# Chunk-selected attention and a top-1 mixture of experts: gate rows on four column tiles, rows beside scales, a one-operation freeze, a reordered prologue, and zero writes at other rounds

## The chip, the cores and the metric

The kernel runs on one core of a Trainium2 chip. Its engines are TensorE (PE, matrix products; PEld is its weight load), VectorE (DVE), ScalarE (ACT), GpSimd (POOL) and SyncE (SP, which here only issues transfers). They run side by side and wait for each other through semaphores. Products go to PSUM[...]; everything else that is computed on lies in SBUF. The metric is the device time of one execution in microseconds (us), lower being better.

## What is computed

The reference is attention over selected chunks, followed by a mixture of experts. Cut to what matters:

```python
# attention: q, k, v are (4, 8, 768, 64)
k_min, k_max = per chunk of 32 keys
ub = sum_d max(q * k_min, q * k_max)          # bound of each query on each chunk
ub = where(causal, ub, -1e9); top_chunks = best 6 of 24
attn = softmax(where(chunk selected and key <= query, q @ k.T / 8, -1e9))
x = (attn @ v) as 3072 tokens of 512
# experts: 8, capacity 80, w1 (512, 1024), w2 (1024, 512)
expert = argmax(x @ w_gate); gate = softmax(x @ w_gate)[expert]
per expert: keep the 80 tokens with the largest gate
out[kept] = gate * (relu(x[kept] @ w1[e]) @ w2[e]);  out[all others] = 0
```

So almost all rows of the output are zero and are written as such; at most 640 rows come from the experts.

## The kernel before, in words

**Tiling.** Four heads make a *quad*; there are 8 quads, two to a batch. The 768 queries of a quad are three tiles t of 256. A *round* is one tile against one pair of key blocks of 128, six rounds to a quad, 48 in all (`rd`, from 0). A tile's last round is an *end*; ends are at r = 0, 2 and 5 of a quad, and each starts a chain of follow-up work, described below.

**A round.** `score(rd)` puts products of rounded queries and keys (`QB`, `KB`) into four PSUM tiles (L459) and adds a large negative penalty to chunks that were not selected (L463, from `PENT` and the indicator `ind`). `exps(rd)` takes exponentials on ACT (L474) and cuts the causal triangle on POOL (L479); `sum_pairs` adds two blocks on POOL (L503) so that the denominators need half of the products. One round later, `value(rd - 1)` multiplies by v (L492, on four column tiles of the array, 32 columns each), `denom(rd - 1)` sums (L517), and at an end `evacuate` copies the numerators to SBUF (L523, `npt`).

**Follow-up of an end.** Two rounds after it `gate_rows` multiplies the numerators by the gate's weights into the PSUM tile that holds the denominators (L530: two products of 128x32 weights by 256 columns, on two column tiles), and ACT copies the result (L534, `DSB`). Three rounds after it `scales` transposes this (L542, `ps_dT`), and VectorE takes reciprocals and scaled gate logits; for the second quad of a batch `best` (L579 to 608) finds the maximum and a one-hot of the expert. Four rounds after it `rows` transposes the numerators (L564, `ps_xn`), scales them into `x_nat` on VectorE (L565) and stores them to `x_dram` through SP (L573). `gates` (L610) finishes the gate weight, and `merges` sort gates in lanes on VectorE (L661 to 722).

**Selection of chunks.** For each quad, `step` transposes k and q on VectorE (L262) and hands rounding and positive parts to POOL (L287) and ACT (L296, L301); `bound_all` and `rank_all` (L390 to 410) bound and rank all chunks, `unselect` (L417) makes the penalty. For quad 0 this is done in thirds in the prologue and in rounds 0 and 1: `keys_third`, `queries_third`, `bound`, `rank` (L355 to 377). The tiles `kT`, `qT`, `qp` have one buffer each, so a quad's first transpose waits until the quad before has been read.

**Freeze.** During rounds 44 to 47 a generator (L735 to 827) chooses the older tokens of batches 0 to 2: a threshold `tau`, prefix counts (`ps_cum`), a one-hot of the slot for each token (L775, 18 operations of 128x80), a product that gathers the kept ones (`ps_old`, L780), a transpose (`ps_gT`) and an exact ranking (`ps_all`). `turn_new` and the three `weigh` steps (L832 to 990) place batch 3's tokens; then the experts' rows are gathered (L1163), multiplied and scattered to `out` (L1205).

**Order and buffers.** The order on each engine is the order in which the program calls the functions, written out by hand (L1028 to 1160), since the planner is switched off there. Small products of all kinds take turns in two PSUM buffers of the pool `psM` (the function `misc`): a product waits until the one before last in that rotation has been read. `late` and `bulk` are lists of small operations that are put off until `flush`. `zero_fill` (L133) writes 512 KB of zeros to the output through SP, twelve times in even rounds 16 to 38. Weights for late experts are read by POOL's queue into tiles that have fallen free (`late_weights`, L999).

## Time and profile before

| | us |
|---|---|
| Median of three runs | 304.55 (301.02 to 305.59) |
| The profiled execution, whole | 302.78 |
| Its span, first to last instruction | 301.1 |
| TensorE busy, of the span | 264.2 (88%) |
| VectorE / ScalarE / GpSimd busy | 200.8 / 154.3 / 196.5 |
| Mean TensorE clock, of full | 0.964 |
| Gate-row products (L530, 96 records) | 15.9 |
| The 18 selection operations (L775) | 4.9 |
| Zero writes (12 of 512 KB), issue to landing | 7.8 each |

All of it but the first row is one execution under the profiler. A group's busy time sums durations that may overlap on TensorE, where tiles of the array run at once, so that records and not instructions are counted there. In the strips of the page a digit is the tenths of a slice of 7.5 us, and the clock strip shows the tenths of full clock that were granted. In a timeline a line has start, duration, engine, line, operation, operands, shapes and count, and in brackets how long the engine had waited and for what.

### The profile page before, as it was taken

Reading aid. Unit: us, or ns where it says so; the run is one execution under the profiler, and the core shown is the slowest. Engines: PE = TensorE matmul, PEld = TensorE weight load, DVE = VectorE, ACT = ScalarE, POOL = GpSimd, SP = SyncE. Lnnn points to the kernel's source line nnn. Section 1 sums busy time; section 2 is a strip of 40 time slices with the busy share of each in tenths; the row PEclk is TensorE's granted clock in tenths of the full one; section 3 lists DMA queues with packets and bytes.
Section 4 is the critical chain, followed back from the end, with each engine's and each line's share of the span. In section 5 each row is a group of like instructions: output and inputs, shape, how many; then the busy total and the mean of one; then the engine's idle time right before and its main releaser. Section 6 shows DMA issues by size and latency. Waiting matters only on the chain.

```text
span 301.1 us, 12164 instructions
## 1 busy us (share of the span) xinstructions
PE 264.2 (88%) x5026; PEld 157.1 (52%) x5026; DVE 200.8 (67%) x747; ACT 154.3 (51%) x352; POOL 196.5 (65%) x398
## 2 busy tenths in 40 slices
PE   8859799979998999799999989997994969789991
PEld 3426456646564666455565545564652544246760
DVE  3849458566746836699877989896989484632431
ACT  1553746934682685567468626856543244403220
POOL 8296695966995885699688739987794401155322
PEclk9999799999999999999999999999998699769999
DMA  7878903999899999999999999966999401112121
GB/s 168 157 191 132 198 6 84 208 166 146 184 204 274 177 217 263 259 190 243 228 272 189 244 257 206 231 102 119 187 214 205 95 3 35 35 44 69 47 65 35
DMA packets 59239, 47.79 MB, mean 159 GB/s; under 512 B 27846, under 2 KB 51526, under 8 KB 59184
## 3 DMA queue, kind: packets, MB, share of 16 engines
q1 hardware_dynamic: 45328, 28.09, 39.6%
q0 software_dynamic: 13536, 18.67, 36.2%
q8 instruction: 39, 0.64, 0.9%
q10 hardware_dynamic: 320, 0.26, 0.3%
q14 instruction: 16, 0.13, 0.1%
HBM read 53.10 MB, written 10.76 MB: 212 GB/s over the span
## 4 chain that ended last, share of the span: by engine, by line
PE 54%; DVE 17%; issue 11%; POOL 7%; ACT 5%; DMA 3%; SPq 2%; POOLq 1%; ACTq 0%; DVEq 0%
PE ps_num L492 20%; PE ps_den L517 8%; PE ps_S L459 6%; PE ps_u L390 6%; ACT E L474 4%; PE ps_den L530 4%; PE ps_xn L564 4%; DVE cand L666 3%; DVE cand L664 3%; PE ps_S L463 2%; POOL X L1163 2%; POOL out_dram L1205 2%; PE ps_dT L542 2%; DVE cand L775 2%; DMA qn<-in_q_dram 1%
## 5 line engine op out<-in xcount | busy, mean ns | idle before, releaser
L474 ACT ACTIVATE E<-ps_S 128x384 f32<-128x384 f32 (+1 forms) x192 | 88.7, 552 | 35.3 <-PE ps_S L463 35.3
L492 PE MATMUL ps_num<-E,vn 128*32 128x256 f32 (+1 forms) x1536 | 94.7, 361 | 3.8 <-issue 3.5
L503 POOL TENSOR_TENSOR both<-E 128x256 f32<-128x256 f32 x92 | 64.5, 731 | 15.6 <-ACT E L474 15.4
L492 PEld LDWEIGHTS ps_num<-E,vn 128*32 128x32 f32 x1536 | 50.4, 111 | 35.3 <-issue 9.7
L479 POOL TENSOR_SCALAR_AFFINE_SELECT E<-E 128x256 f32<-128x256 f32 x96 | 42.3, 468 | 34.0 <-ACT E L474 34.0
L459 PE MATMUL ps_S<-QB,KB 32*128 32x256 bf16 (+1 forms) x768 | 35.2, 261 | 3.0 <-ACT E L474 1.5
L534 ACT ACTIVATE DSB<-ps_den 128x256 f32<-128x256 f32 x24 | 9.2, 384 | 41.3 <-PE ps_den L530 37.8
L463 PE MATMUL ps_S<-PENT,ind 32*128 32x256 bf16 (+1 forms) x384 | 24.9, 255 | 2.5 <-DVE PENT L377 2.5
L459 PEld LDWEIGHTS <-KB 32*128 32x128 bf16 x768 | 17.2, 94 | 15.7 <-issue 12.5
L287 POOL CAST KB<-kT 128x768 bf16<-128x768 f32 (+1 forms) x18 | 23.9, 1336 | 0.0
L517 PE MATMUL ps_den<-E,ones 128*32 128x256 f32 (+1 forms) x400 | 23.6, 332 | 0.1
L565 DVE TENSOR_TENSOR x_nat<-ps_xn,rec 128x512 bf16<-128x512 f32 x24 | 16.4, 684 | 7.9 <-PE ps_xn L564 5.0
L402 DVE STREAM_TRANSPOSE ub<-ps_u 128x160 f32<-128x160 f32 x28 | 7.4, 316 | 18.3 <-PE ps_u L390 18.3
L517 PE MATMUL ps_den<-both,ones 128*32 128x256 f32 x184 | 19.2, 380 | 0.0
L296 ACT ACTIVATE qp<-qT 128x640 f32<-128x640 f32 (+2 forms) x20 | 12.6, 640 | 12.7 <-DVE qT L262 12.6
L262 DVE STREAM_TRANSPOSE kT<-kn 128x768 f32<-128x768 f32 (+1 forms) x17 | 15.6, 919 | 4.3 <-DMA kn<-in_k_dram 3.9
L564 PE MATMUL ps_xn<-ident_f,npt 128*128 128x128 f32 x96 | 16.1, 291 | 2.2 <-DVE sm L619 1.5
L664 DVE MAX8 cand<-cand 64x8 f32<-64x128 f32 (+3 forms) x40 | 13.7, 343 | 6.1 <-ACT cand L677 5.2
L517 PEld LDWEIGHTS ps_den<-E,ones 128*32 128x32 f32 x400 | 12.8, 109 | 8.9 <-issue 3.9
L523 ACT ACTIVATE npt<-ps_num 128x512 f32<-128x512 f32 x24 | 14.6, 608 | 4.9 <-PE ps_num L492 4.8
L1205 POOL DMA_INDIRECT out_dram<-Y,sidx x8 | 7.4, 923 | 14.8 <-DVE Y L1203 14.8
L279 DVE TENSOR_REDUCE KMM<-kT 128x24 f32<-128x768 f32 (+1 forms) x20 | 15.8, 792 | 1.5 <-PE ps_u L355 1.0
(241 smaller groups left out, 458.8 us busy)
## 6 DMA issues: line engine op xcount, KB each, us to landing
w<-in_moe_w_dram POOLq DMA_DIRECT2D x11, 1024.0 KB, 11.9
out_dram<-zero_tile SPq DMA_DIRECT2D x12, 512.0 KB, 7.8
kn<-in_k_dram SPq DMA_DIRECT2D x28, 192.0 KB, 5.2
qn<-in_q_dram SPq DMA_DIRECT2D x28, 192.0 KB, 6.2
vn<-in_v_dram SPq DMA_DIRECT2D x28, 192.0 KB, 5.5
x_dram<-x_nat SPq DMA_DIRECT2D x12, 257.0 KB, 4.8
kn<-in_moe_w_dram POOLq DMA_DIRECT2D x1, 768.0 KB, 8.3
qn<-in_moe_w_dram POOLq DMA_DIRECT2D x1, 768.0 KB, 12.6
```

Source lines behind the costliest of these rows:

```text
L287: nc.gpsimd.tensor_copy(out=straight(KB[s][:, f, ts]), in_=natural(kT[:, f, ts]))
L390: nc.tensor.matmul(out=tiles[h][32 * j:32 * (j + 1), :, :], lhsT=KMM[s][rs, w, f, :], rhs=x[rs, j], start=(w == 0 and f == 0), stop=(w == ...
L459: nc.tensor.matmul(out=ps_S[h][:, m, 0:wid], lhsT=KB[s][rs, w, keys], rhs=QB[s][rs, w, q0:q0 + wid], start=(w == 0), stop=False, skip_grou ...
L463: nc.tensor.matmul(out=ps_S[h][:, m, lo - q0:wid], lhsT=ind[rs, keys], rhs=PENT[s][rs, lo - NFULL:q0 + wid - NFULL], start=False, stop=Tru ...
L474: nc.scalar.activation(out=E[:].rearrange("p m q -> p (m q)")[:, 0:last], in_=ps_S[h][:].rearrange("p m q -> p (m q)")[:, 0:last], func=my ...
L479: nc.gpsimd.affine_select(out=diag, in_=diag, compare_op=ALU.is_ge, fill=0.0, base=0, pattern=[[0, 2], [1, 4], [4, CHUNK]], channel_multip ...
L492: nc.tensor.matmul(out=NUM[q0:q0 + 32, a, c0:THIRD], lhsT=nats[(g, "vn")][:, kb, 2 * a + r, 32 * f:32 * (f + 1)], rhs=Es[rd][2 * a + r][:, ...
L503: nc.gpsimd.tensor_tensor(out=both[:], in0=E[:, 0, :], in1=E[:, 1, :], op=ALU.add)
L517: nc.tensor.matmul(out=dn[32 * h:32 * (h + 1), c0:THIRD], lhsT=ones32[:], rhs=src, start=(i == 0 and m == 0), stop=False, skip_group_check ...
L564: nc.tensor.transpose(ps_xn[:, j, a, :], npt[:, a, j * P:(j + 1) * P], ident_f32[:])
L565: nc.vector.tensor_tensor(out=xbuf[(b, t)][:, :, P * gi:P * (gi + 1)].bitcast(BF16).rearrange("p j (k d) -> p j k d", d=HEAD_D), in0=ps_xn ...
L664: nc.vector.max(out=top, in_=src)
```

## The change

1. `gate_rows` makes four products of 128 columns on four column tiles in place of two of 256 on two; the second half of the columns lands 64 partitions lower, and the reading of `ps_dT` follows that.
2. `rows` is called directly after `scales`, three rounds after an end, then `best`; the store of `x_nat` is issued after `gates`.
3. In `freeze` one `tensor_tensor` of 128x1440 makes the one-hot.
4. The prologue's order is new: `ind`, `edge` and `ones32` are built later, the first keys are rounded on POOL rather than ACT, the query thirds round at once, the third key and query transposes come right after the second, filler products (`busy`) replace `idle(5)`, round 0 is finished (value, sums, evacuation) before score 1, the third bound and rank of quad 0 move from round 1 to round 2, behind step K0 of quad 1, whose other steps move to round 3. Constants for the selection are built at rounds 16 and 22.
5. Zero writes go to rounds 5, 6, 33, 34, 45, 46 and 47. Half of one expert's second weights no longer lies in the tile of zeros, but is read at round 44 into the v tile of quad 6.

```diff
             def keys_third(i):
-                cs = slice(2 * i, 2 * (i + 1))
-                turn(kT, kn, slice(8 * i, 8 * (i + 1)), slice(0, 2))
-                for f in range(2):
-                    widths, ordered = keys(f, cs)
+                parts = [keys(f, slice(2 * i, 2 * (i + 1))) for f in range(2)]
+                if i == 0:
+                    for _, ordered in parts:
+                        ordered()
+                for widths, ordered in parts:
                     widths()
                     if i:
                         late.append(ordered)
...
             def queries_third(i):
...
+                parts = [queries(f, slice(2 * i, 2 * (i + 1))) for f in range(2)]
+                for which in range(2):
+                    for part in parts:
+                        part[which]()
...
         def gate_rows(g, t):
             gi = g % 2
             dn = DEN[:, (3 * g + t) % 2, :]
-            for a in range(2):
-                nc.tensor.matmul(out=dn[32 * a:32 * (a + 1), :], lhsT=wgx[:, 2 * gi + a, :],
-                                 rhs=nps[(g, t)][:, a, :], start=False, stop=True,
-                                 skip_group_check=True)
+            for j in range(2):
+                for a in range(2):
+                    tile_of = slice(32 * (2 * j + a), 32 * (2 * j + a + 1))
+                    ts = slice(P * j, P * (j + 1))
+                    nc.tensor.matmul(out=dn[tile_of, ts], lhsT=wgx[:, 2 * gi + a, :],
+                                     rhs=nps[(g, t)][:, a, ts], start=False, stop=True,
+                                     skip_group_check=True)
...
-            for c in range(OLDB):
-                nc.vector.tensor_scalar(out=sel[:, c, :], in0=slot1[:], scalar1=slot[:, c:c + 1],
-                                        scalar2=None, op0=ALU.is_equal)
+            each = [P, OLDB, CAP]
+            nc.vector.tensor_tensor(out=sel, in0=slot1[:, None, :].to_broadcast(each),
+                                    in1=slot[:, :, None].to_broadcast(each), op=ALU.is_equal)
...
+        def busy(n):
+            ps = misc([P, THIRD], F32, "ps_busy")
+            for _ in range(n):
+                nc.tensor.matmul(out=ps[:], lhsT=PENT[1][:, 0:P], rhs=PENT[1][:, 0:THIRD],
+                                 start=True, stop=True, skip_group_check=True)
...
-                load_parts(5, 1, [bf(nats[(7, "kn")][:]), bf(zt[:])])
+                load_parts(5, 1, [bf(nats[(7, "kn")][:])])
...
+                load_parts(5, 1, [vspace[:, 4 * DMOD:6 * DMOD]])
...
-        steps_of = {1: ["K0"], 2: ["K1", "Q0"], 3: ["Q1"], 6: ["K0", "K1"], 7: ["Q0"], 8: ["Q1"]}
+        steps_of = {2: ["K0"], 3: ["K1", "Q0", "Q1"], 6: ["K0", "K1"], 7: ["Q0"], 8: ["Q1"]}
...
+        fills = {5: 2, 6: 2, 33: 1, 34: 1, 45: 2, 46: 2, 47: 2}
...
+            nc.gpsimd.memset(PEN[0][:], 0.0)
+            build_indicator(cand[1][:, 0:SEQ])
             u = prep(0)
             units = [u]
+            u["turn"]("K", 0)
             u["K"](0)
+            build_edge()
+            u["turn"]("Q", 0)
             u["Q"](0)
-            flush()
             u["bound"](1, 2)
-            idle(5)
+            u["turn"]("K", 1)
             u["K"](1)
             u["rank"](1, 2)
+            u["turn"]("Q", 1)
             u["Q"](1)
-            build = {0: build_constants, 1: build_projection, 3: build_selection, 4: build_ties}
+            u["turn"]("K", 2)
+            u["turn"]("Q", 2)
+            busy(10)
+            build = {0: build_constants, 16: build_selection, 22: build_ties}
...
-                if rd - 4 in ends:
-                    rows(*ends[rd - 4])
                 if rd - 3 in ends:
                     eg, et = ends[rd - 3]
                     scales(eg, et)
+                    rows(eg, et)
+                    if eg % 2:
+                        best(eg // 2, et)
...
                 if rd == 0:
                     units[0]["bound"](2, 4)
-                    units[0]["K"](2)
                     units[0]["rank"](2, 4)
                     units[0]["Q"](2)
-                elif rd == 1:
-                    units[0]["bound"](4, 6)
-                    units[0]["rank"](4, 6)
+                    units[0]["K"](2)
+                    busy(5)
+                    finish(0)
+                    busy(5)
...
+                if rd == 3:
+                    flush()
...
+                if rd == 2:
+                    units[0]["bound"](4, 6)
+                    units[0]["rank"](4, 6)
-                if 1 <= rd < N:
+                if 1 < rd < N:
                     value(rd - 1)
```

## The prediction

> **What bounds the kernel now.** I read the page first: busy totals, the strip of 40 slices, and the engines of the chain that ended last.

> ```profile
> span 301.1 us, 12164 instructions
> PE 264.2 (88%) x5026; PEld 157.1 (52%) x5026; DVE 200.8 (67%) x747; ACT 154.3 (51%) x352; POOL 196.5 (65%) x398
> ...
> PE   8859799979998999799999989997994969789991
> ...
> PEclk9999799999999999999999999999998699769999
> ...
> PE 54%; DVE 17%; issue 11%; POOL 7%; ACT 5%; DMA 3%; SPq 2%; POOLq 1%; ACTq 0%; DVEq 0%
> ```

> TensorE is the bound. Its timeline has gaps over 0.3 us of 34.6 us in all, and its clock dips after two of them: slice 5 (30 to 40 us, prologue) and slices 31 and 35 (the freeze). Between lies a steady part, one quad every 27.5 us, in which PE hardly waits. So an edit pays if it (a) shortens PE's own work in the steady part, (b) removes a gap, or (c) saves a clock dip. The windows give the dips, the columns after the busy times of PE, PEld, DVE, ACT and POOL being clock, DMA share and GB/s:

> ```profile
> 30.00:35.00 5.00, 3.34 (x55) 2.13 (x48) 3.21 (x6) 3.54 (x7) 2.24 (x4) 0.87 0.96 217
> 35.00:40.00 5.00, 5.00 (x153) 2.91 (x149) 0.00 (x0) 3.63 (x8) 4.73 (x16) 0.78 0.46 88
> 230.00:240.00 10.00, 7.51 (x93) 4.55 (x92) 5.54 (x24) 2.78 (x9) 3.31 (x10) 0.66 0.76 140
> ```

> Lost to the clock: 5×0.13 + 5×0.22 = 1.75 us and 10×0.34 = 3.4 us. PE's list of waits names the stalls (total, times, longest):

> ```profile
> PE ps_old L780 <- DVE x_nat L565: 2.9, 1, 2.9
> PE ps_S L463 <- DVE PENT L377: 2.5, 2, 1.6
> ...
> PE ps_xn L564 <- DVE sm L619: 1.5, 1, 1.5
> ...
> PE ps_dT L542 <- DVE oh L606: 1.4, 2, 0.7
> ```

> And the timelines show the pieces that the change touches: one gate-row pair, the 18-op selection and PE's wait behind it, POOL and VectorE around the third rank.

> ```profile
> 53.47 0.41 PE L530 MATMUL ps_den<-npt,wgx 128*32 128x256 f32 x2
> ...
> 225.41 4.75 DVE L775 TENSOR_SCALAR cand<-slot,slot 128x80 bf16<-128x80 bf16 x17
> ...
> 230.96 0.83 PE L780 MATMUL ps_old<-slotrhs,cand 128*80 128x48 bf16 x18 [2.93 <-DVE x_nat L565]
> ...
> 19.45 2.77 POOL L503 TENSOR_TENSOR both<-E 128x256 f32<-128x256 f32 x4
> 22.17 1.21 POOL L287 CAST KB<-kT 128x256 bf16<-128x256 f32 x2
> 22.38 0.45 DVE L367 STREAM_TRANSPOSE ub<-ps_u 128x256 f32<-128x256 f32 x1 [3.90 <-PE ps_u L355]
> 25.02 0.94 DVE L262 STREAM_TRANSPOSE kT<-kn 128x768 f32<-128x768 f32 x1
> ```

> [...] (0.87 and 0.78 behind the 1.09 us gap at 31.65, 0.66 in the freeze), but the 3.7 us of gaps between 15 and 21 us cost no clock, so no gap length settles it. [...] 32 value matmuls on four tiles take 1.51 us though one is 0.36. [...]

> **Part by part**, against the profiled execution: 302.78 us, span 301.1 and 1.7 around it. That is 1.8 below the median shown (304.55; runs 301.02 to 305.59).

> *Gate rows.* A full round of scores, values and sums takes 2.30 us without the pair (46.76 to 49.06) and 2.72 with it (53.47 to 56.19): 0.42. A diagonal one takes 2.23 without (70.63 on) and 2.50 with it (49.83 to 52.33): 0.27. The pair uses two of four column tiles; four matmuls of 128 columns should take half the stream, 0.21 to 0.25. Gain 0.04 to 0.2 each, times 24: −1 to −4.5. I take −3. It is PE work in PE-bound rounds, so nothing hides it.

> *Rows with scales.* The PE work is the same; what moves is the order in the two misc PSUM buffers and on VectorE. Before, scales came directly behind another end's rows and its ps_dT waited for best() of the tile before, 0.73 us at 139.65 and 0.63 at 195.03. Now at those two places (rounds 27 and 39) ps_xn waits for a best() that VectorE reaches 0.68 us (one x_nat, the mean of L565) later. I price this at +0.85 each, +1.7 in all; bounds +0.5 and +3. At the other 22 ends, rows' PSUM is free: its last tenant is released by x_nat or a copy queued earlier. Stores go behind gates(), but only the last waits there: SP issued store (3,2) at 258.06, the gather starts at 265.29 behind VectorE's index work. Zero.

> *Freeze.* 18 operations, 4.90 us of VectorE, become one of 1,440 results a lane. Estimate: [...] from L961, 0.49×4.5 = 2.2. I take 1.8, a saving of about 3.1. What is late next: ps_old needs the selection and, by the misc rotation, x_nat of (7,0). x_nat of (6,2) now lies ahead of tau, +0.7. By hand, ps_old starts at 229.1, not 230.96; score 46 follows at 229.9, not 234.4, since the 1.53 us wait of ps_xn at 231.79 and its 1.09 us of transposes are gone from there. The second exact ranking (ps_all) then starts at 234.9, not 239.7, if the clock holds: 4.8 us; about 3 if it falls again. Against it, round 47: ps_xn waits for the four ranks of L814, and ps_n starts 5.1 us after ps_all, not 4.0: +1.05. Rows at the end (0.65 us and a 0.62 gap) go: −0.5. Sum −3.5; bounds −5 and −1.5.

> *Prologue.* Gone: 15.78 to 17.94 is shortened by building `ind` later and turning K2/Q2 early, and the 3.82 us for which ACT waited on qT before 31.46. Added: 20 filler matmuls, which run where PE waited, so nothing if the wait ends no earlier. The price is the third rank. In the changed order VectorE does K0 of unit 1 ahead of it, and K0 writes the kT buffer, which POOL's cast of key third 2 must have read. On POOL that cast now stands behind select(0), key third 1's casts, the constants (with a 0.63 memset and a 0.66 projection), the widths and the 2.77 us of pair sums. Walking POOL with durations of before: 16.8, 18.0, 20.05, 21.7, 24.5, casts end 25.7 (23.4 before). K0 on VectorE to 28.6; rank to 31.35 (25.1 before); the mask of score 3 at 31.4, not about 28.4. PE idles about 3.3 us around 27 to 31, so the clock probably dips. On the other side K1, Q0, Q1 end by 37.1, exps of 4 at 39.8, the bounds of unit 1 at 39.25, its ranks at 43.15. Score 6 would start at 44.5 instead of 46.21 (−1.7) with a full clock, at 46.2 to 47.6 (0 to +1.4) with the dip. I take −0.5; bounds −3 and +2.

> *Zero fills.* Twelve 512 KB writes leave rounds 16 to 38. SP runs ahead of the engines, so four issue at about 35 us, where the DMA strip falls empty until 49, and two each at about 168 and 199 us. Four follow store (3,0) at about 231 and end by 248 (2 MB at 200 GB/s), before store (3,2) and long before the scatter at 276. On the path: nothing. If the cover went, the gather would wait for up to 10 us of writes. Inside the steady part they were near three "issue" stalls (1.61 at 66.06, 1.40 at 90.70, 1.61 at 120.64) which no engine explains. I count −1; bounds −2 and +1. The weight half that moves to round 44 has until expert 5, after 280 us: zero.

> Sum: −0.5 −3 +1.7 −3.5 −1 = −6.3, so 296.5 us.

> **The rivals.**

> *B, both dips go.* With PE kept busy in the prologue and score 46 earlier, neither stage loses clock: the prologue gives −3, the freeze −5, gate rows −4: 302.8 −3 −4 +1.7 −5 −1 = 291.5. For: the freeze's two largest waits go. Against: the new gap behind K0.

> *C, the gains are eaten.* Clock falls at both places and gate rows were mostly hidden in the pipelining of column tiles: +1.5 −1 +1.7 −2 −0.5 = −0.3, so 302.5. For: the fall in the trace needs little more than a 1 us gap behind others. Against: 0.42 is measured in a round with no other difference.

> *D, slower: misc PSUM as bound.* scales and rows now take both misc buffers back to back at every end. If ps_xn waits for the reader of the tile before it at all 24 ends, not two, for the 0.68 us that ps_dT waited, this is 24×0.68 = 16.3 instead of 1.7: 302.8 −8.0 +16.3 = 311. It decides from (8.0+6.1)/24 = 0.59 us an end. For: ps_dT waited 0.73 and 0.63 on the same rotation. Against: half of the ends have no best(), and PE has a whole round between the tenants.

> *E, the change doesn't do what it says:* the freeze's operation is short but ps_old still waits for x_nat, as its releaser in the line above says. Then the freeze gives −1.5: 298.5.

> **How the numbers follow.** Chances: forecast 0.42 (293.5 to 299.5), E 0.10, B 0.15, C 0.20, D 0.13. The range holds 290 to 304: the forecast's case with B, C and E; what is left out is D and the far ends of B and C. A measurement of this kernel tells about 2% from no change, 6.1 us, so the bound is 296.7 on the profiled execution's scale and 298.5 on the median's. Faster: B 0.15, two thirds of the forecast's 0.42 (the scale being in doubt by those 1.8 us), a little of E: 0.45. Slower: D with a tail of C: 0.14. Same: the rest, 0.41.

> **What would show it.** Right: [...] ps_old at about 229 less what was gained before it; PE rounds with a gate pair at about 2.5; four concurrent gate matmuls; rank(4,6) at about 31 with PE idle before score 3; waits of ps_xn on best's output near rounds 27 and 39; a clock near 1.0 in the freeze. Wrong: the spacing of the steady quads not below 27.2; ps_xn waiting at most ends; a clock dip longer than before; the store or the gather behind zero fills.

## The result: 3.2% slower, and the profile after

The changed kernel takes 312.63 us (median of 4 runs, 310.89 to 313.54), the kernel before 303.47 (301.02 to 305.59): a ratio of 1.032, 95% interval 1.023 to 1.042. The forecast was 296.5, at most 304. A later comparison gave 1.029 (1.022 to 1.037). Ratios here and below are taken over the executions within 1.5% of their kernel's fastest, so they need not equal the ratio of the medians.

The page of the changed kernel, the lines that answer to those shown of before, and one of the table of transfer queues (packets, MB, share of 16 engines' span):

```profile
span 311.8 us, 12359 instructions
...
PE 265.5 (85%) x5136; PEld 161.0 (52%) x5137; DVE 198.1 (64%) x730; ACT 153.5 (49%) x350; POOL 198.0 (64%) x400
...
PE   8788879979898997999789979995798767769992
...
PEclk9989978998999999899979989998799999979997
...
q8 instruction: 40, 0.66, 0.9%
...
PE 42%; DVE 21%; issue 13%; POOL 10%; DMA 5%; ACT 4%; SPq 2%; POOLq 1%; ACTq 0%; DVEq 0%
```

TensorE is as busy as before (265.5 us, it was 264.2) in a longer span: the loss is idle time and, within the busy time, a lower clock. The clock strip has holes all along (slices 6, 17, 21, 24 and 28, counted from 1), where before had them in the prologue and the freeze alone. Its list of waits:

```profile
PE ps_S L463 <- issue: 5.3, 2, 3.7
PE ps_num L492 <- issue: 3.2, 1, 3.2
...
PE ps_num L492 <- POOL E L479: 2.3, 3, 0.9
...
PE ps_den L517 <- issue: 1.9, 1, 1.9
...
PE ps_S L459 <- issue: 1.7, 1, 1.7
...
PE ps_den L517 <- POOL E L479: 1.4, 1, 1.4
...
PE ps_xn L568 <- DVE oh L611: 0.7, 2, 0.5
```

and the lines of the same kind in the kernel before, of which the prediction named three stalls and set them beside the zero writes:

```profile
PE ps_num L492 <- issue: 3.5, 3, 1.6
PE ps_u L390 <- issue: 2.2, 3, 1.4
...
PE ps_num L492 <- POOL E L479: 0.3, 1, 0.3
```

"issue" means that nothing which the profile shows was awaited. Stalls of this kind over 0.3 us rose from 5.4 to 12.1 us. Waits for GpSimd rose from 0.3 to 3.7. The wait that I had priced for rows beside scales (ps_xn on best's output) is 0.7 in all.

By stage, each from the start of the named product to the next; ps_tau is the threshold's product at the start of the freeze, ps_idx the index product at its end (score 6 at 46.21 and 49.73, score 40 at 202.54 and 212.45, ps_tau at 221.26 and 237.94, ps_idx at 263.83 and 275.53):

| stage | before | after | difference | forecast |
|---|---|---|---|---|
| to score 6 | 46.2 | 49.7 | +3.5 | -0.5 |
| score 6 to 40 | 156.3 | 162.7 | +6.4 | -2.3 for both |
| score 40 to ps_tau | 18.7 | 25.5 | +6.8 | |
| freeze, to ps_idx | 42.6 | 37.6 | -5.0 | -3.5 |
| rest | 37.3 | 36.3 | -1.0 | 0 |

So in these two profiles the freeze did better than forecast, and the loss lies ahead of it. Its selection is now one operation, and the gate rows' records cover 11.4 us, not 15.9 (groups of the changed kernel: busy, mean ns, idle before):

```profile
L780 DVE TENSOR_TENSOR cand<-slot,slot 128x1440 bf16<-128x1440 bf16 x1 | 1.7, 1660 | 0.0
...
L533 PE MATMUL ps_den<-npt,wgx 128*32 128x128 f32 x192 | 11.4, 313 | 0.2 <-ACT npt L523 0.2
```

The largest single loss, in the timeline of the changed kernel around score 41:

```profile
211.66 0.86 PE L517 MATMUL ps_den<-E,ones 128*32 128x256 f32 x16
212.45 0.73 PE L459 MATMUL ps_S<-QB,KB 32*128 32x256 bf16 x8
...
217.05 0.30 PE L463 MATMUL ps_S<-PENT,ind 32*128 32x128 bf16 x4 [3.65 <-issue]
```

TensorE stops in the middle of one score's products, all of whose operands are there. Just before it stand the 128 bound products of a quad (L390), and just before those, bulk transfers were issued by GpSimd and SyncE:

```profile
207.66 0.83 POOL L153 DMA_DIRECT2D w<-in_moe_w_dram  x1
...
208.39 1.01 SPq L139 DMA_DIRECT2D out_dram<-zero_tile  x2
```

The windows show what follows, the clock (column after the five engines) falling to 0.75 and 0.78. The last line is 40 to 50 us of the kernel before:

```profile
40.00:50.00 10.00, 8.27 (x158) 4.58 (x134) 8.52 (x34) 2.77 (x5) 2.94 (x5) 0.75 0.57 212
...
210.00:220.00 10.00, 6.34 (x189) 3.97 (x165) 6.20 (x40) 2.73 (x7) 4.12 (x13) 0.78 0.95 206
```
```profile
40.00:50.00 10.00, 9.44 (x219) 5.66 (x213) 7.73 (x33) 5.01 (x10) 7.76 (x12) 1.00 0.04 8
```

In the clock's own records the stretches at half speed add up to 15.0 us before and 30.7 after, counted up to ps_idx. TensorE was busy in 13.0 and 29.1 us of them, so that up to 8 us more of its work was lost to the clock. In both profiles each whole stretch between two changes of the clock is a multiple of 3.41 us (those at half speed 3.41, 6.83 or 10.24), and TensorE was busy for 0.7 to 2.2 of the 3.41 us ahead of each of these falls, so a stall of less than 2 us, with other gaps near, came before some of them.

```
stalls without a releaser over 0.3 us                              104
of these at position 192 to 196 modulo 256                         103
from the landing of the last instruction packet to the restart     0.98 to 1.71 us, median 1.44
```

Every stall but one, in kernels with different work at that place, lies at one of five neighbouring positions modulo 256, which I take for the border of a block, and ends about 1.4 us after a packet of 16 KB has landed (in the changed kernel: 43.43 and 44.84, 155.44 and 156.89, 215.64 and 217.05). From this I infer that TensorE was waiting for its own instructions: 5.4 us of such waits before, and 12.1 after.

The traces also show when a block was late. The packet that ended a stall started only after TensorE had crossed the border before. Over all borders of the 20 profiles, the packet ahead of a border started in the median 0.5 us after that earlier crossing where the DMA engines were less than 30% busy until it landed (143 borders), and 2.6 us after it where they were over 90% busy (475 borders). TensorE stalled where it ran through the block in less time than this delay, the packet's 1 us or so (0.98 in the median of the changed kernel) and the 1.44 us after it take together: this sum tells stall from no stall at 734 of the 749 borders that lie less than 15 us behind the one before.

### The profile page after: what moved, and what is told of

It is laid out like the page before. It is cut to its first block, busy times and chain, and to the rows that moved or that the text cites. A ratio compares the mean times of both kernels' runs of the same rounds, so it can differ in the third digit from the quotient of the medians.

```text
span 311.8 us, 12359 instructions
## 1 busy us (share of the span) xinstructions
PE 265.5 (85%) x5136; PEld 161.0 (52%) x5137; DVE 198.1 (64%) x730; ACT 153.5 (49%) x350; POOL 198.0 (64%) x400
## 4 chain that ended last, share of the span: by engine, by line
PE 42%; DVE 21%; issue 13%; POOL 10%; DMA 5%; ACT 4%; SPq 2%; POOLq 1%; ACTq 0%; DVEq 0%
PE ps_num L492 16%; PE ps_den L517 6%; PE ps_S L459 5%; PE ps_u L390 5%; DVE cand L671 4%; DVE cand L669 3%; POOL both L503 3%; DMA vn<-in_v_dram 3%; ACT E L474 2%; PE ps_xn L568 2%; POOL out_dram L1243 2%; PE ps_S L463 2%; PE ps_den L533 2%; POOL X L1201 2%; DVE x_nat L569 2%
## 5 line engine op out<-in xcount | busy, mean ns | idle before, releaser
L492 PE MATMUL ps_num<-E,vn 128*32 128x256 f32 (+1 forms) x1536 | 91.6, 375 | 5.4 <-issue 3.2
L503 POOL TENSOR_TENSOR both<-E 128x256 f32<-128x256 f32 x92 | 64.1, 727 | 28.8 <-ACT E L474 28.5
L492 PEld LDWEIGHTS ps_num<-E,vn 128*32 128x32 f32 x1536 | 48.9, 116 | 36.5 <-issue 12.7
L459 PE MATMUL ps_S<-QB,KB 32*128 32x256 bf16 (+1 forms) x768 | 37.0, 263 | 5.0 <-DVE ub L402 1.9
L463 PE MATMUL ps_S<-PENT,ind 32*128 32x256 bf16 (+1 forms) x384 | 26.1, 260 | 7.4 <-issue 5.3
L547 DVE RECIPROCAL rec<-ps_dT 128x8 f32<-128x8 f32 x24 | 4.8, 200 | 36.8 <-PE ps_dT L545 36.7
L289 POOL CAST KB<-kT 128x768 bf16<-128x768 f32 (+1 forms) x20 | 25.4, 1279 | 0.1
L264 DVE STREAM_TRANSPOSE kT<-kn 128x768 f32<-128x768 f32 (+1 forms) x17 | 15.7, 923 | 10.2 <-DMA vn<-in_v_dram 6.3
L402 DVE STREAM_TRANSPOSE ub<-ps_u 128x160 f32<-128x160 f32 x28 | 7.3, 315 | 15.9 <-PE ps_u L390 15.9
L517 PE MATMUL ps_den<-both,ones 128*32 128x256 f32 x184 | 16.0, 405 | 1.4 <-POOL E L479 1.4
L568 PE MATMUL ps_xn<-ident_f,npt 128*128 128x128 f32 x96 | 15.1, 281 | 2.3 <-DVE rec L547 1.2
L463 PEld LDWEIGHTS <-ind 32*128 32x128 bf16 x384 | 12.3, 95 | 9.1 <-issue 8.2
## 6 DMA issues: line engine op xcount, KB each, us to landing
qn<-in_moe_w_dram POOLq DMA_DIRECT2D x1, 768.0 KB, 12.1
```

The lines of the kernel that those rows point to most:

```text
L264: nc.vector.transpose(out=dst[:, fs, 32 * xs.start:32 * xs.stop].rearrange("p f (x t) -> p x f t", t=CHUNK), in_=src[:].rearrange("p c (i ...
L289: nc.gpsimd.tensor_copy(out=straight(KB[s][:, f, ts]), in_=natural(kT[:, f, ts]))
L459: nc.tensor.matmul(out=ps_S[h][:, m, 0:wid], lhsT=KB[s][rs, w, keys], rhs=QB[s][rs, w, q0:q0 + wid], start=(w == 0), stop=False, skip_grou ...
L463: nc.tensor.matmul(out=ps_S[h][:, m, lo - q0:wid], lhsT=ind[rs, keys], rhs=PENT[s][rs, lo - NFULL:q0 + wid - NFULL], start=False, stop=Tru ...
L492: nc.tensor.matmul(out=NUM[q0:q0 + 32, a, c0:THIRD], lhsT=nats[(g, "vn")][:, kb, 2 * a + r, 32 * f:32 * (f + 1)], rhs=Es[rd][2 * a + r][:, ...
L503: nc.gpsimd.tensor_tensor(out=both[:], in0=E[:, 0, :], in1=E[:, 1, :], op=ALU.add)
```

## The experiments

Theory F: blocks of instructions come late when a border falls near the 128 bound products (256 records in 3 us) while bulk transfers fill the DMA engines; adding instructions moves the borders. Theory W: the loss is in waits of rows beside scales. Theory P: it is in the new prologue. Times are compared within a chip, for a reason given at the end; where a reading crosses chips, the text says so.

**One part at a time.** The four kernels are the kernel before with some of the diff's hunks: gate rows and freeze; rows, best and stores; the whole prologue; the zero writes.

```diff
+            for j in range(2):
+                for a in range(2):
+                    tile_of = slice(32 * (2 * j + a), 32 * (2 * j + a + 1))
...
+            nc.vector.tensor_tensor(out=sel, in0=slot1[:, None, :].to_broadcast(each),
```

> The kernel before with two parts of the change alone: gate rows on four column tiles and the one-operation selection in the freeze. Theory F (the loss comes from late blocks of TensorE's own instructions, which share the DMA engines with bulk transfers): the 48 more gate products move the block borders by a little, the transfers are as before, so the two parts show their own worth: gate rows -0.5 to -3, freeze -3 to -5, together 296 to 300 us, with 4 to 8 us of stalls without a releaser on TensorE. Theory W (the loss comes from waits of the misc PSUM buffers behind best, once rows stand beside scales): the same 296 to 300, since rows are where they were. Theory P (the new prologue alone costs the 10 us): the same.

```diff
-                if rd - 4 in ends:
-                    rows(*ends[rd - 4])
...
+                    rows(eg, et)
+                    if eg % 2:
+                        best(eg // 2, et)
```

> The kernel before with rows beside scales (and best and the stores behind them) alone. Theory W: most of the 10 us loss is here, 309 to 313 us, and TensorE's waits for ps_xn or ps_dT on best's output exceed 8 us in all. Theory F: within 3 us of before, 300 to 306, waits for ps_xn on best under 2 us in all; if it is longer, then by stalls without a releaser on TensorE. Theory P: no change.

```diff
+            u["turn"]("K", 2)
+            u["turn"]("Q", 2)
+            busy(10)
...
+        steps_of = {2: ["K0"], 3: ["K1", "Q0", "Q1"], 6: ["K0", "K1"], 7: ["Q0"], 8: ["Q1"]}
```

> The kernel before with the new prologue alone. Theory P: 310 us or more, with score 7 later than before by 3 us and more lost after it through the order that the prologue leaves. Theory F: score 7 starts at 49 to 50.5 us (before: 49.06), the rest shifts with the block borders, 301 to 308 us. Theory W: within 2 us of before.

```diff
+        fills = {5: 2, 6: 2, 33: 1, 34: 1, 45: 2, 46: 2, 47: 2}
```

> The kernel before with the zero writes at their new rounds alone. Theory F: four writes of 512 KB at about 35 us stand in the DMA engines when TensorE runs the 128 bound products of quad 1, so a stall without a releaser of 1.5 to 2 us appears there, and another near 208 us; the stalls that the old writes made go. 301 to 309 us. Theories W and P: no change, 301 to 306, with no new stall.

Measured ratios: 1.002 (0.998 to 1.006), 1.004 (1.000 to 1.007), 1.009 (1.005 to 1.013), 1.001 (0.998 to 1.003). No part costs 3% on this chip. The changed kernel as a whole was never timed there, so W and P have to be judged by the runs below. Stalls without a releaser: 10.8, 4.9, 8.7 and 7.6 us. The first missed the gain of some 2% that all three theories had forecast: the freeze did gain (score 44 to ps_idx in 40.8 us, 44.5 before), but the stalls, 5 us more, can account for its loss. In the last, a stall of 1.8 us came at 45 us behind the four early writes, as forecast. None came near 208, and against the forecast the three old stalls stayed at their borders (1.9, 2.0 and 1.6 us), though the writes had moved away.

**The changed kernel again, and both without bulk transfers in the loop.** The first two kernels are unchanged. In the other two every weight load and zero write is put off until the attention part is over; the loads of k, q and v stay:

```diff
     def load_parts(e, which, spaces):
+        put_off.append(lambda: load_now(e, which, spaces))
...
             weigh2()
+            for run in put_off:
+                run()
```

> The kernel before, unchanged, on the chip of this comparison, for its profile. If the long gap of TensorE at the start of the experts that the four runs of single parts showed (6.1 to 6.5 us ahead of L1186) is the chip's and not the parts', it is here too, and the execution takes 308 to 316 us.

> The changed kernel, unchanged, on the same chip as the runs of single parts. If the parts add up, it is 1.5% above before (+0.2 +0.4 +0.9 +0.1). Theory F: 1.01 to 1.04, since the stalls depend on where block borders meet transfers and don't add up. Theory W: 1.03 again. In its profile the gap ahead of L1224 tells whether the experts' stage loses as much as before's does on this chip.

> The kernel before with all weight loads and zero writes put off to the end of the attention part (so the experts wait for them, and the whole takes some 60 to 80 us longer; the measure is when the freeze's index product, ps_idx, starts, 263.8 us in the first profile). Theory F: with bulk transfers gone from the loop, blocks of instructions come in time: stalls without a releaser on TensorE fall from 5.4 us to under 1.5, and ps_idx starts at 252 to 259 us. Theories W and P: stalls of that kind may stay; ps_idx within 3 us of the first profile.

> The changed kernel with the same transfers put off. Theory F: stalls without a releaser fall from 12.0 us to under 1.5, and ps_idx starts 2 to 7 us earlier than in the kernel before with the same transfers put off, as the sum of the parts in the prediction had it. Theory W: the change still loses, ps_idx 5 us or more later than there. Theory P: later by 3 us, all of it before score 7.

These four ran on one chip, but not on that of the parts, as the expectation has it. Before took 306.33 in its single run, with no long gap at the experts, so that question stayed open. After: 1.029 again. The parts come to 1.5% together, but on the other chip, so it is not shown that they fail to add up. Without bulk transfers ps_idx starts at 261.1 us in the kernel before and at 258.0 in the changed one: the sign turns, from 5.6 us later (267.4 and 273.0 with transfers, same chip) to 3.1 earlier. Each is one profile, and in these the clock was at half speed for 21.9 us of the kernel before and 10.2 of the changed one up to ps_idx, so the size of the 3.1 is uncertain. The whole takes 394.68 and 392.69 us. The kernel before then has one such stall, the changed one still several (lines of their wait lists):

```profile
PE ps_u L397 <- issue: 0.8, 1, 0.8
```
```profile
PE ps_den L524 <- issue: 1.3, 1, 1.3
PE ps_num L499 <- issue: 1.2, 1, 1.2
PE ps_S L466 <- issue: 1.1, 1, 1.1
```

F holds for the sign, and the stalls fall from 6.1 to 0.8 and from 11.1 to 3.9 us on the same chip. Two of its forecasts failed: ps_idx of the kernel before was to start at 252 to 259 us, and the changed kernel's stalls were to fall under 1.5 us (3.9). The blocks ahead of its four stalls ran through in 2.6 to 4.5 us, so blocks run through that fast stalled TensorE, for up to 1.3 us, even so. Score 6 is at 46.7 and 47.1: without the early writes the new prologue is nearly as fast as the old one, so P falls as the main cause.

**Moving the borders.** Same work, but 16 of the 24 warm-up products become 64 smaller ones, which shifts all that follows by 96 instructions; the second kernel also splits the 20 fillers (136); the last applies the 96 to the kernel before.

```diff
-            idle(24)
+            idle(8)
+            for _ in range(64):
+                nc.tensor.matmul(out=NUM[:, 0, 0:P], lhsT=PENT[1][:, 0:P], rhs=PENT[1][:, 0:P],
+                                 start=True, stop=True)
```

> The changed kernel with the same work, but TensorE's instruction stream shifted by 96 instructions: of the 24 warm-up products at the start 16 are made as 64 smaller ones, in a stretch where TensorE waits anyway. Theory F: each stall without a releaser again lies at a border of 256 instructions (position 13 modulo 256 when counted from record 180), and the borders now fall at 202, 212, 64, 171, 21, 126 and 232 records after the start of the bound products of quads 1 to 7 (42, 52, 160, 11, 117, 222 and 72 before the shift). So the stalls of quads 1, 2 and 7 (1.7 to 3.7 us) go, and new ones come in quads 3, 5 or 6; the total moves by up to 6 us either way. Theory W, and a rival that the stalls belong to certain instructions: the stalls stay in the same rounds, 311 to 313 us.

```diff
-            for _ in range(n):
-                nc.tensor.matmul(out=ps[:], lhsT=PENT[1][:, 0:P], rhs=PENT[1][:, 0:THIRD],
+            for _ in range(2 * n):
+                nc.tensor.matmul(out=ps[:, 0:P], lhsT=PENT[1][:, 0:P], rhs=PENT[1][:, 0:P],
```

> The changed kernel shifted by 136 instructions (the warm-up products as in the shift by 96, and the 20 fillers of the prologue made as 40 of half the width). Borders then lie 162, 172, 24, 131, 237, 86 and 192 records after the start of the bound products of quads 1 to 7. Theory F: positions between 126 and 232 showed no or small stalls, so only quads 3 and perhaps 5 and 6 stall, in all under 6 us; 299 to 305 us, at or below before. Theory W, or the rival that the loss is in the parts themselves: 308 or more.

> The kernel before shifted by 96 instructions in the same way. Its borders then lie 249, 28, 158, 32, 161, 33 and 161 records after the start of the bound products of quads 1 to 7 (89, 124, 254, 128, 257, 129 and 257 before the shift). Theory F: the stalls at 380 and 254 records of quads 2, 3 and 4 go, and new ones appear at 284 to 290 records in quads 2, 4 or 6, and none in 3, 5 and 7; the time may move by 4 us either way. The rival that stalls belong to certain instructions: same rounds, same time.

```
                       stall in us (records after the start of the bound products) in quads 1 to 7
before                 -          0.3 (124)  1.4 (254)  1.6 (384)  -          0.5 (130)  -
                                  1.6 (380)
before, shifted 96     -          0.8 (284)  0.5 (158)  4.5 (288)  1.0 (417)  3.7 (290)  0.7 (417)
                                             0.9 (414)
after                  1.7 (298)  1.6 (308)  -          1.9 (268)  3.2 (374)  -          3.7 (328)
after, shifted 96      -          1.7 (212)  3.7 (320)  1.7 (427)  1.6 (278)  -          -
                                                                   0.5 (789)
after, shifted 136     -          1.6 (172)  3.8 (280)  2.2 (388)  -          0.4 (342)  0.9 (450)
```

Each row is one profile. A second profile of the changed kernel has its five stalls at the same five borders, with 3.2, 1.0, 0.5, 3.3 and 3.1 us: the places repeat, the sizes don't.

The shift by 96 takes the changed kernel from 1.029 to 1.008 (0.999 to 1.017, same chip), with stalls gone from quads 1 and 7, new ones in 3 and 5, and quad 4's at the next border. Quad 2's was to go and stayed, at the same border, which now lies 96 records earlier in the work. Shifted by 136 it is at 1.000 (0.995 to 1.004) and has 8.9 us of stalls, where under 6 were forecast; that is on another chip, where the unshifted one was not timed, so how much of it is the shift's doing is not shown. The kernel before becomes 2.7% slower (1.018 to 1.035) by 96 instructions that cost no time where they stand: its stalls in quads 4 and 6, in the shifted kernel's wait list,

```profile
PE ps_xn L564 <- issue: 8.2, 2, 4.5
```

fall on transposes that did not stall in the kernel before. A rival in which stalls belong to certain instructions is out, and one in which the whole loss belongs to the parts cannot explain why the kernel before slows down without any of them. Forecasts by position alone were half right (quads 3, 5 and 7 of this kernel were to have none), since a position says nothing of what the DMA engines carry then.

**Moving the transfers instead.** Weight loads at rounds 4 and 6 of a quad rather than 2 and 4, in both kernels, and in one with the zero writes moved too:

```diff
-                if r in (2, 4) and 1 <= g <= NPRE or r == 2 and g == NPRE + 1:
-                    load_whole(g - 1, r // 2 - 1)
+                if r == 4 and 1 <= g <= NPRE + 1:
+                    load_whole(g - 1, 0)
+                if r == 0 and 2 <= g <= NPRE + 1:
+                    load_whole(g - 2, 1)
```

> The changed kernel with each quad's two weight loads of 1 MB issued at its rounds 4 and 6 instead of 2 and 4, so that none stands in the DMA engines when the 128 bound products of round 3 run through a block of instructions in 3 us. Theory F: the stalls of quads 4, 5 and 7 (1.9, 3.2, 3.7 us) shrink to 1.5 or less, with the clock that followed; those of quads 1 and 2 stay. 302 to 307 us. Theory W: no change, 310 to 313.

```diff
+        fills = {35: 2, 47: 6}
...
+                if rd == 5:
+                    for _ in range(4):
+                        zero_fill(filled.pop(0), nc.scalar)
```

> As the run before it, and also the zero writes moved: four issued by ScalarE after the exponentials of round 5 (behind the first bound products instead of ahead of them), two at round 35, six at round 47. Theory F: the stall of quad 1 goes too, score 6 starts at 47 to 48 us instead of 49.7, and the whole takes 298 to 304 us, at or below the kernel before. Theory W: 309 to 313.

> The kernel before with the weight loads moved in the same way and nothing else. Theory F: its stalls without a releaser (5.4 to 6.1 us) shrink too, but less, since they are smaller and its zero writes stay in the loop: 298 to 303 us. Theory W: no change.

All three missed: 1.025 (1.009 to 1.040), 1.041 (1.034 to 1.048), 1.040 (1.029 to 1.050), with stalls of 14.5, 11.7 and 12.9 us, one of them 5.7. The loads landed no sooner over all (medians of 10.1 to 12.1 us; 9.8 to 11.9 in the two profiles each of both kernels unmoved); that they now met those of k, v and q is likely, not shown. The kernel before has the same TensorE instructions either way, and its stalls went from 6.1 to 12.9 us: moving the transfers alone changed the size of the stalls, but my picture of when the DMA engines are free was wrong. Only the early writes' part held: behind round 5 they let score 6 start at 46.1. Score 7 then waited 1.7 us for a mask (PENT, L419) that ScalarE made only behind its four transfers, and started at 50.8 us.

**What else is in the loss.** The changed kernel shifted by 136 with the early writes on ScalarE, and with rows back in the fourth round:

```diff
+        fills = {33: 1, 34: 1, 45: 2, 46: 2, 47: 2}
...
+                        zero_fill(filled.pop(0), nc.scalar)
```

> The same with the first four zero writes issued by ScalarE behind the exponentials of round 5, so that they follow quad 1's bound products. Theory F: score 6 at 46 to 47 us as with the shift alone if quad 1's border no longer meets the writes; within 2 us of the run beside it. If the early writes cost more than that one stall [...], 2 to 4 us faster than it.

```diff
+                if rd - 4 in ends:
+                    rows(*ends[rd - 4])
...
-                    rows(eg, et)
```

> The changed kernel shifted by 136, with rows and stores back in round 4 after an end as before. Theory F with the waits on GpSimd as a cost of rows beside scales (0.9 us at rounds 12, 24 and 36): they shrink to 0.3 each, the two waits of ps_dT on best (0.7) come back, the freeze loses 1 to 2 us; within 2 us of a_s136. Theory W: 4 us or more faster than it.

Ratios 1.008 (1.005 to 1.011) and 1.001 (0.997 to 1.005), beside 1.000. Once quad 1's border is elsewhere, moving the writes gains nothing: the kernel is 0.8% slower, and its score 7 waits 1.5 us for the same mask. With rows back, the waits for GpSimd fall from 3.3 to 0.8 us, the freeze does not lose the 1 to 2 us forecast (38.7 and 39.6), and nothing is gained or lost over all: W has no weight. Those waits, in the changed kernel's timelines of TensorE and GpSimd,

```profile
82.39 1.86 PE L492 MATMUL ps_num<-E,vn 128*32 128x256 f32 x28 [0.92 <-POOL E L479]
```
```profile
80.41 1.51 POOL L289 CAST KB<-kT 128x768 bf16<-128x768 f32 x1
81.88 1.69 POOL L479 TENSOR_SCALAR_AFFINE_SELECT E<-E 128x256 f32<-128x256 f32 x4
```

come with rows beside scales: they are 0.3 us before and 1.7 with rows alone. The lines show how: TensorE comes to values whose exponentials GpSimd cuts only after a cast. That it comes sooner because rows left that round is the likely reason, not a tested one.

**A version that keeps the borders.** The freeze's operation alone, and the same with rows beside scales, add no TensorE instruction.

```diff
-            for c in range(OLDB):
-                nc.vector.tensor_scalar(out=sel[:, c, :], in0=slot1[:], scalar1=slot[:, c:c + 1],
+            nc.vector.tensor_tensor(out=sel, in0=slot1[:, None, :].to_broadcast(each),
```

> The kernel before with the one-operation selection alone. It adds no instruction to TensorE, so the block borders stay where they were. Theory F: the stalls stay at 5 to 7 us in the rounds of before, and the freeze gains what its profile showed in the run with gate rows (some 3 to 4 us between score 44 and the index product): ratio 0.985 to 0.993. If the gain is taken back by the waits that follow in the freeze, 0.995 to 1.005.

> The same with rows, best and stores moved beside scales, which adds no TensorE instruction either, and moves 8 of them ahead of the bound products. Theory F: the selection's wait for x_nat goes as well, 1 to 2 us faster than the run beside it: ratio 0.978 to 0.990. If rows beside scales cost more in the rounds (waits on GpSimd, 0.7 to 0.9 us each) than they gain in the freeze: 0.990 to 1.000.

0.990 (0.984 to 0.996) and 0.986 (0.979 to 0.994), medians 301.70 and 301.97 where before has 304.57: 1.0 and 1.4% faster, while the changed kernel was 3% slower than before wherever it was timed (not on this chip). What rows add to the freeze's operation, forecast at 1 to 2 us, is not clear of the noise. Stalls are 5.8 and 3.8 us, in quads 2 to 4, where before has its own.

## Why the prediction was wrong

- **Gate rows, -3.** The size holds. With gate rows and the freeze alone, rounds 1, 2 and 4 of a quad take 3.44, 4.11 and 3.49 us in quads without a stall, where before has 3.64, 4.29 and 3.69; round 1 of quads 2, 4 and 6 gains nothing. Over the 24 ends this is an estimated -2 to -4. What failed is that the added records, 96 of products and 96 of weight loads, were counted by their time alone. They move every later border, and gate rows with the freeze came out at 1.002.
- **Rows with scales, +1.7.** The waits of ps_xn on best's output are 0.7 us in all, in place of 1.4 of ps_dT before. Against that stand waits for GpSimd, 3.4 us more in the changed kernel and 1.4 more with rows alone, which "rows' PSUM is free" didn't ask about. Rows alone came out at 1.004.
- **Freeze, -3.5.** Right in mechanism, and about right in size. The operation took 1.66 us, 1.8 forecast, which was my estimate, below the 2.2 that the 0.49 us of a 128x320 operation (L961 before) gives for 1,440 columns. From ps_tau to ps_old it is 6.9 us, not 9.7, and ps_old no longer waits, so E is out. From ps_tau to ps_idx the first profile gives -5.0, with a mean clock of 1.00 there in the changed kernel; in the second profile the gain is 2.1. Over all profiles the stage takes 37.5 to 42.4 us with the one operation and 42.5 to 43.5 without.
- **Prologue, -0.5.** +3.5 with the early writes. Its own steps were near: the third rank ended at 30.05 (31.35 forecast), TensorE waited 0.90 for it (3.3 forecast), and with transfers put off it is 0.4 slower than the old one.
- **Zero writes, "on the path: nothing", and -1 for issue stalls.** This is the step that turned the sum. The prediction saw three stalls that no engine explained and put them down to the writes near by, so it expected them to shrink; stalls of this kind rose from 5.4 to 12.1 us. By the test above they were late instruction blocks: all three lie at position 193 modulo 256 and end 1.23 to 1.44 us after a packet has landed. The first of the three, at 66.06 us, came before any zero write (the first was issued at 87.45), and with the writes moved alone all three stayed. The four early writes, put into the very gap of the DMA strip that was called free, stood ahead of such a block, as the lines under this list show, and the clock was at half from 44.95 to 48.36 us. The same border also stalled 1.1 us with weight loads and zero writes put off and 1.5 us with the prologue alone, so the writes made a stall longer that the new order had brought there.
- **The sum.** Stalls +6.7, clock up to +8 and GpSimd +3.4 stand against the freeze's -5.0 and the gate rows' -3. They overlap in part, so this is no exact account. The 34.6 us of gaps in the prediction contain some 6 us behind the last product. D, the slower rival, had the wrong mechanism: ps_xn waited for best at two ends of 24.

```profile
37.37 3.39 SPq L139 DMA_DIRECT2D out_dram<-zero_tile  x4
```
```profile
44.84 0.34 PE L459 MATMUL ps_S<-QB,KB 32*128 32x256 bf16 x2 [1.73 <-issue]
```

## What to carry to other kernels

Read the releaser "issue" of the bounding engine before anything else. Here 103 of 104 of its stalls lay at multiples of 256 records, from which I infer that the engine waited for its own program, and edits redrew them: the kernel before had 5.4 and 6.1 us of stalls in its two profiles, 12.1 with its instructions shifted by 96, and 12.9 with its weight loads moved by two rounds. Price an edit that adds such instructions or moves a transfer with a range of both signs as wide as the stalls that are there (here 5 us, and they went up to 14.5), and compare versions by shifting the stream, or with transfers put off, before judging an edit. Where the gain of a part matters, take first the parts that add no instruction to that engine.

## What the runs showed of the hardware that was not expected

A shift of TensorE's instructions by 96, with no other work, made one kernel 2.7% slower and another 2% faster, each against runs on the same chip. The longest wait for a block was 5.7 us, in the changed kernel with weight loads and zero writes moved. In the eight profiles taken on two of the chips, the experts' first result came 13.9 to 14.7 us after the first ps_XT, where it is 6.3 to 6.4 on the others (with transfers in the loop), and the kernel before had a median of 312.1 and 312.4 us there, 303.5 to 304.6 elsewhere. The line for it, from the kernel with rows beside scales alone:

```profile
PE ps_H L1189 <- ACT XT L1178: 7.1, 2, 6.5
```

TensorE waits for ScalarE, whose first copy of ps_H starts 5.8 us after that product there and at once in the kernel before; what ScalarE waits for the trace does not name, and nothing was tried. The kernel before was not profiled on those chips; the changed kernel unshifted was timed on neither.
